# A gated mix of cached attention and an MLP on one core: the last row of wo on each partition is loaded early by GpSimd in seven loads of unequal size

## The chip, the cores and the metric

The kernel runs on one core of one Trainium2 chip. The engines of a core are TensorE (PE in the profile), VectorE (DVE), ScalarE (ACT), GpSimd (POOL) and SyncE (SP); each has its own program, and they meet only at semaphores. Loads from the chip's memory (HBM) are issued by an engine's program and carried out by the core's 16 DMA engines. The metric is the device time of one launch in microseconds.

## The reference

One token attends to a cache of 32,768 positions; 32 query heads share 8 key-value heads, four to one. Beside it a gated MLP runs on the same token, and a sigmoid gate mixes the two. All is float32.

```python
x = A_x                                               # 1 x 1 x 512
g = _sigmoid((x * gate_w).sum(-1, keepdims=True))
q = (x @ wq).reshape(B, Sq, 32, 128)                  # per head
...
scores = jnp.einsum("bhqd,bhkd->bhqk", q, k) * (Dh ** -0.5)
p = _softmax(scores, axis=-1)
o = jnp.einsum("bhqk,bhkd->bhqd", p, v)
a = o.transpose(0, 2, 1, 3).reshape(B, Sq, 4096) @ wo # wo is 4096 x 512
...
b = (_silu(x @ w1) * (x @ w3)) @ w2                   # 512 -> 1792 -> 512
return g * a + (1 - g) * b
```

The two caches hold 2 x 8 x 32,768 x 128 floats, 268 MB; wq and wo hold 8.4 MB each, w1, w2 and w3 3.7 MB each.

## The kernel before

Three buffers of 8 MB, `ra`, `rb` and `rc`, take turns for everything that is loaded. Each has 64 KB on each of the 128 partitions, and a load fills a whole buffer, so each partition gets one piece of 64 KB. SP issues all the large loads in an order written out by hand (lines 133 to 166): wq, w1 and w3 first, then for each of the eight key-value heads two halves of K (into `ra` and `rb`) and two halves of V (into `rc`). Before each load SP waits on a count (`c_k` for scores done, `c_v` for values done) that says that TensorE is through with the buffer's last content.

For each head DVE transposes the K pieces in place (line 368), PE computes the scores (298), ACT copies them out of PSUM (406), PE turns them (322), DVE and PE find the maxima, ACT computes the exponentials into `prob` (412), and in the next turn of the loop PE multiplies them with V (312). The result of a head goes through ACT into `ob`, a tile of 512 floats per partition (409), from where PE sums it with `fold` (332, `heads`). GpSimd's only work in the loop is to place the queries of the next head in `winbuf` (285): it waits until the scores of the head before are done, copies four times, and signals `t_win`, for which PE waits at the start of a turn.

The last stage begins when the last V half has been used. `wo` is seen as 128 partitions with 32 rows of 512 floats each (row 32p + k lies on partition p as its k-th piece). It is loaded into `rc` in two halves of 16 rows, with the semaphores `l_wo0` and `l_wo1` (line 157). w2 follows into `ra` as five loads of 7, 4, 2, and twice half a row (163 and 166, semaphores `l_w20` to `l_w24`). PE runs 32 multiplications with wo (444), waiting for `l_wo0` before the first and `l_wo1` before the 17th, then those with w2 (451 and 423), each group behind its semaphore; between them it adds in the wo part by way of ACT, `ob` and `fold` (477 and 423). DVE and ACT copy the result out of PSUM (485) and ACT stores it (489).

`ob` also holds x at the start of the kernel (`xr`), and the sigmoid of the MLP's gate (268). `prob` is 1,040 floats wide: columns 0 to 511 are the weights of the first V half, 512 to 1023 those of the second.

Of the kernel before, what the change touches and what calls it, by code (L numbers as in the profile page):

```python
# [9 lines left out]
PE, DVE = mybir.EngineType.PE, mybir.EngineType.DVE  # L10

P = 128


class Count:
# [11 lines left out]
@with_exitstack  # L27
def kernel(ctx, tc, x, k_cache, v_cache, wq, wo, w1, w3, w2, gate_w, out):
    nc = tc.nc
    rb, rc = (nc.alloc_sbuf_tensor(n, [P, 16384], F32).ap() for n in ("rb", "rc"))  # L30
    l_q, l_w1, l_w3 = (nc.alloc_semaphore(n) for n in ("l_q", "l_w1", "l_w3"))
    loads = [(rc, wq, l_q)]
    n = w1.shape[0] * w1.shape[1] // P
    loads += [(rb[:, i * n:(i + 1) * n], w, sem) for i, (w, sem) in enumerate(((w1, l_w1), (w3, l_w3)))]
    for to, w, sem in loads:
        i = nc.sync.dma_start(to, w.rearrange("(p c) n -> p (c n)", p=P)).then_inc(sem, 16)

        tc.no_tile_sem_insts.add(i.ins.name)
    tc.close()
    tc.compile()  # L40
    _program(nc, rb, rc, l_q, l_w1, l_w3, x, k_cache, v_cache, wq, wo, w1, w3, w2, gate_w, out)


def _program(nc, rb, rc, l_q, l_w1, l_w3, x, k_cache, v_cache, wq, wo, w1, w3, w2, gate_w, out):
    pe, dve, act, pool, sp = nc.tensor, nc.vector, nc.scalar, nc.gpsimd, nc.sync
    _, HKV, S, DH = k_cache.shape
    D = x.shape[-1]
    F = w1.shape[1]
    HQ = wq.shape[1] // DH
    REP = HQ // HKV  # L50
    NC = D // P
    FR = F // P
    FJ = F // 4
    SCALE = DH ** -0.5
    NK = S // (2 * P)
    W = NK * DH
    assert DH == P and D == 4 * P and REP == 4 and HKV == 8 and NK == 128 and F == FR * P

    def sb(name, *shape):
        return nc.alloc_sbuf_tensor(name, [P, *shape], F32).ap()  # L60

    def token(name):
        return nc.alloc_semaphore(name)

    def count(name):
        return Count(nc, name)
# [9 lines left out]
    winbuf = sb("winbuf", 4 * 32 + 16)  # L76
    sbuf = sb("sbuf", 16, 32, 2)
    prob = sb("prob", 1024 + 16)
    ob = sb("ob", 512)
    otall = sb("otall", REP + HQ)  # L80
    oq = sb("oq", 64)
    gsm, gate = sb("gsm", 1), sb("gate", 2)
# [3 lines left out]
    flat = sbuf.rearrange("p a i m -> p (a i m)")  # L86
    omask = flat[:, 0:P]
    hid = flat[:, P:P + FJ]
    htp = sb("htp", FR, 32)

    xr, gp = ob[0:1, 0:D], flat[0:1, D:2 * D]
    gr = prob[0:1, 0:8 * (D // 8 + 2)].rearrange("o (k d) -> o k d", k=8)[:, :, 0:D // 8]

    zero, row = flat[32:33, 0:D], prob[0:1, 0:D]
# [15 lines left out]
    l_v = [token(f"l_v{i}") for i in range(2)]  # L110
    l_wo = [token(f"l_wo{i}") for i in range(2)]
    l_w2 = [token(f"l_w2{i}") for i in range(5)]

    c_q, c_k, c_v, c_e = (count(n) for n in ("c_q", "c_k", "c_v", "c_e"))
    c_nm, c_act, c_pool, done = token("c_nm"), count("c_act"), count("c_pool"), count("done")
# [10 lines left out]
    def take(sem, n=1, engine=pe):  # L126
        engine.wait_ge(sem, n).then_inc(sem, -n)  # L127
# [4 lines left out]
    half = W // 2  # L132
# [21 lines left out]
    wod = wo.rearrange("(p k) e -> p (k e)", k=32)  # L154
    sp.wait_ge(c_v.sem, 2 * HKV - 2)
    for i in range(2):
        sp.dma_start(rc[:, i * half:(i + 1) * half], wod[:, i * half:(i + 1) * half]).then_inc(l_wo[i], 16)
    w2t = ra[:, 0:FR * D].rearrange("p (k e) -> p k e", e=D)
    w2d = w2.rearrange("(p k) e -> p k e", k=FR)
    W2 = (0, 7, 11, 13, 14)  # L160
# [3 lines left out]
    for i in range(2):  # L164
        e = slice(i * D // 2, (i + 1) * D // 2)
# [36 lines left out]
    @contextmanager  # L202
    def ahead(name, mark, left, right):

        pe.br_lt(left, right, on_true=f"{name}_end", on_false=f"{name}_body").branch_hint(mark)
        with nc.body(f"{name}_body", valid_engines=[PE]):
            yield
            pe.br(f"{name}_end")
        nc.switch_bb(f"{name}_end")
# [3 lines left out]
    for c in range(NC):  # L213
        m = pe.matmul(  # L214
            mc[:, NC + c:NC + c + 1], xr.rearrange("o (p c) -> o c p", c=NC)[:, c], ones[0:1, 0:1],
            start=True, stop=True,
# [8 lines left out]
    for c in range(NC):  # L225
        for b in range(2):
            for j in range(4):
# [3 lines left out]
                    start=(c == 0), stop=(c == NC - 1),  # L231
# [46 lines left out]
    for h in range(HKV):  # L278
        if h:
            pool.wait_ge(c_k.sem, 2 * h)  # L280
        else:
            pool.wait_ge(c_act.sem, n_win)
            pool.wait_ge(c_pool.sem, c_pool.n)
        for r in range(4):
            pool.tensor_copy(  # L285
                winbuf[32 * r:32 * r + 32, 16:144].rearrange("p (c k) -> p c k", k=32)[:, :, 4 * r:4 * r + REP],
                winraw[32 * r:32 * r + 32, h],
            ).then_inc(t_win, 1)


    def scores(m, region, first, last):
# [127 lines left out]
    acc, pb = s_ps[1], s_ps[0]  # L419

    def rows(lhs, rhs, start=False, stop=False, quarters=range(4)):
        for j in quarters:
            i = pe.matmul(  # L423
                pb[32 * j:32 * j + 32, 0:P], lhs, rhs[:, j * P:(j + 1) * P], start=start, stop=stop
            )
        return i
# [11 lines left out]
    with ahead("fifth", marks[4], zero_reg, 0):  # L438
        take(t_e)
        for k in range(32):  # L440
            if k % 16 == 0:
                pe.wait_ge(l_wo[k // 16], 16)
            t = k % 4
            pe.matmul(  # L444
                acc[32 * t:32 * t + 32, :], oq[:, k:k + 32], rc[:, k * D:(k + 1) * D], start=(k < 4), stop=False,
                skip_group_check=True,
            )
        pe.wait_ge(l_w2[0], 16)
        for k in range(W2[1]):
            t = k % 4  # L450
            i = pe.matmul(  # L451
                acc[32 * t:32 * t + 32, :], htp[:, k, :], w2t[:, k, :], start=False, stop=(k >= W2[1] - 4),
                skip_group_check=True,
            )
        i.then_inc(c_e.sem, 1)
        for i in range(1, 3):
            pe.wait_ge(l_w2[i], 16)
            for k in range(W2[i], W2[i + 1]):
                rows(htp[:, k, :], w2t[:, k, :], start=(k == W2[1]))
                if k == W2[2] - 1:  # L460
                    take(t_e)
                    rows(fold, ob)
# [61 lines left out]
```

## Time and profile before

| what | us |
|---|---|
| median of 3 runs | 691.83 (691.78 to 691.87) |
| the profiled execution's own time | 691.74 |
| its span, first to last instruction | 690.4 |
| PE busy | 349.7 |
| DVE busy | 306.9 |
| ACT busy | 41.6 |
| POOL busy | 7.0 |
| bytes moved, mean rate | 296.36 MB, 429 GB/s |

The span is what the trace shows between the first and the last instruction; 1.34 us of the execution's own time lie around it. The first table of the profile gives busy time by engine, a second one the span in 40 slices, where a digit of 9 is a share of 90% or more.

### The profile page before, as it was taken

What the parts mean: (1) busy time and instruction counts of PE and PEld (TensorE: products, weight loads), DVE (VectorE), ACT (ScalarE), POOL (GpSimd) and SP (SyncE); (2) the same over time, 40 slices, a digit from 0 to 9 for tenths busy, and PEclk for the clock granted to TensorE, in tenths of its full rate; (3) what the DMA queues carried; (4) which work ended last, traced back from release to release, by engine and by line L of the source; (5) the groups of instructions that cost most, each with busy time, mean ns of one, the idle gap of its engine ahead of it and who ended that gap; (6) DMA issues with size and microseconds to landing.
All of it is one profiled execution on the core that took longest, in us unless ns stands there. A gap on an engine that the chain in (4) does not pass through costs nothing. (4 is left out here: it accounts for less than half of the span.)

```text
span 690.4 us, 6719 instructions
## 1 busy us (share of the span) xinstructions
PE 349.7 (51%) x2946; PEld 112.6 (16%) x2946; DVE 306.9 (44%) x194; ACT 41.6 (6%) x111; POOL 7.0 (1%) x41
## 2 busy tenths in 40 slices
PE   1721645757065721757066721766075712766567
PEld 1200103103011120203021220203021210203122
DVE  1015862991725447091825447091815446191000
ACT  0110011002000010002000010002000010002000
POOL 0000000000000000000000000000000000000000
PEclk9985675988578965889567965988578965878679
DMA  9999999999999999999999999999999999999997
GB/s 414 393 469 426 425 426 427 444 448 429 426 425 440 425 437 452 429 429 425 437 429 429 456 433 429 425 433 433 425 444 444 430 429 425 437 429 429 452 411 320
DMA packets 6079, 296.36 MB, mean 429 GB/s; under 512 B 691, under 2 KB 947, under 8 KB 1078
## 3 DMA queue, kind: packets, MB, share of 16 engines
q1 hardware_dynamic: 6048, 296.23, 99.3%
q8 instruction: 6, 0.10, 0.1%
q14 instruction: 3, 0.02, 0.0%
q10 hardware_dynamic: 22, 0.01, 0.0%
HBM read 296.23 MB, written 0.00 MB: 429 GB/s over the span
## 5 line engine op out<-in xcount | busy, mean ns | idle before, releaser
L368 DVE STREAM_TRANSPOSE rb<-rb 128x2048 f32<-128x2048 f32 x64 | 141.8, 2275 | 130.7 <-DVEq L127 130.7
L312 PE MATMUL psum<-rc,prob 128*32 128x512 f32 x896 | 114.9, 671 | 140.5 <-PEq L127 140.5
L368 DVE STREAM_TRANSPOSE ra<-ra 128x2048 f32<-128x2048 f32 x64 | 141.3, 2274 | 58.3 <-DVEq L127 58.3
L298 PE MATMUL psum<-rb,winbuf 128*32 128x512 f32 x512 | 88.8, 771 | 84.9 <-PEq L127 84.9
L298 PE MATMUL psum<-ra,winbuf 128*32 128x512 f32 x512 | 60.9, 614 | 26.7 <-PEq L127 21.2
L312 PEld LDWEIGHTS psum<-rc,prob 128*32 128x32 f32 x896 | 34.2, 122 | 216.0 <-issue 216.0
L392 DVE TENSOR_REDUCE mx<-psum 128x4 f32<-128x1024 f32 x8 | 9.8, 1225 | 86.9 <-DVEq L127 86.9
L298 PEld LDWEIGHTS psum<-rb,winbuf 128*32 128x32 f32 x512 | 13.0, 120 | 159.1 <-issue 159.1
L406 ACT COPY sbuf<-psum 128x512 f32<-128x512 f32 x16 | 9.9, 616 | 471.1 <-PE psum L298 471.1
L298 PEld LDWEIGHTS psum<-ra,winbuf 128*32 128x32 f32 x512 | 16.8, 112 | 69.4 <-issue 69.4
L412 ACT ACTIVATE prob<-psum,nm 128x256 f32<-128x256 f32 x32 | 18.8, 693 | 47.0 <-DVE nm L400 47.0
L322 PE MATMUL psum<-ident,sbuf 128*64 128x64 f32 x512 | 18.1, 234 | 5.0 <-PEq L127 5.0
L322 PEld LDWEIGHTS psum<-ident,sbuf 128*64 128x64 f32 x512 | 17.0, 148 | 12.5 <-issue 12.5
L373 DVE SCALAR_TENSOR_TENSOR otall<-psum,gate,recip 128x4 f32 (+1 forms) x8 | 1.7, 214 | 33.3 <-DVEq L127 33.3
L345 PE MATMUL psum<-sums,ones 128*128 128x4 f32 x16 | 4.5, 350 | 22.8 <-PEq L127 22.8
L312 PE MATMUL psum<-rb,prob 128*32 128x512 f32 x64 | 8.8, 714 | 9.4 <-DMA rb<-in_A_v_cache_dram 9.4
L312 PE MATMUL psum<-ra,prob 128*32 128x512 f32 x64 | 9.9, 790 | 3.5 <-DMA ra<-in_A_v_cache_dram 3.5
L285 POOL COPY winbuf<-winraw 32x16 f32<-32x16 f32 x32 | 6.1, 190 | 535.7 <-PE psum L298 501.5
L444 PE MATMUL psum<-rc,oq 128*32 128x512 f32 x64 | 9.0, 712 | 3.9 <-DMA rc<-in_A_wo_dram 3.5
L229 PE MATMUL psum<-rc,xp 128*32 128x512 f32 x64 | 8.4, 687 | 4.7 <-DMA rc<-in_A_wq_dram 4.7
L256 PE MATMUL psum<-rb,xp 128*32 128x448 f32 x64 | 7.8, 637 | 5.4 <-DMA rb<-in_B_w_dram 5.3
L214 PE MATMUL psum<-ones,ob 1*128 1x1 f32 x8 | 2.0, 370 | 15.1 <-DMA prob<-in_gate_w_dram 15.1
(62 smaller groups left out, 86.4 us busy)
## 6 DMA issues: line engine op xcount, KB each, us to landing
rc<-in_A_wo_dram SPq DMA_DIRECT2D x2, 4096.0 KB, 45.8
rb<-in_B_w_dram SPq DMA_DIRECT2D x2, 3584.0 KB, 34.1
ra<-in_B_w_dram SPq DMA_DIRECT2D x1, 1792.0 KB, 33.0
ra<-in_B_w_dram SPq DMA_DIRECT2D x1, 1024.0 KB, 35.2
ra<-in_B_w_dram SPq DMA_DIRECT2D x1, 512.0 KB, 35.9
ra<-in_B_w_dram SPq DMA_DIRECT2D x2, 128.0 KB, 35.7
rc<-in_A_v_cache_dram SPq DMA_DIRECT2D x14, 31.1
ra<-in_A_k_cache_dram SPq DMA_DIRECT2D x8, 41.5
```

The source lines that it names most:

```text
L229: m = pe.matmul(pq[b][32 * j:32 * j + 32, :], xp[:, c, :], rc[:, o:o + REP * DH], start=(c == 0), stop=(c == NC - 1),)
L256: i = pe.matmul(ps[32 * j:32 * j + 32, 0:FJ], xp[:, c, :], rb[:, o:o + FJ], start=(c == 0), stop=(c == NC - 1))
L285: pool.tensor_copy(winbuf[32 * r:32 * r + 32, 16:144].rearrange("p (c k) -> p c k", k=32)[:, :, 4 * r:4 * r + REP], winraw[32 * r:32 * r + ...
L298: i = pe.matmul(s_ps[m][32 * g:32 * g + 32, :], winbuf[:, w:w + 32], region.rearrange("p (n c i) -> p c n i", c=4, i=32)[:, c, n:n + 16], ...
L312: i = pe.matmul(o_ps[32 * t:32 * t + 32, :], prob[:, w:w + 32], region[:, n * DH:(n + 4) * DH], start=(r == 0 and g == 0 and f == 0), stop ...
L322: i = pe.matmul(pf[64 * s:64 * s + 64, 64 * a:64 * a + 64], sbuf[:, a].rearrange("p i m -> p (i m)"), ident.rearrange("p (gf r s q) -> p s ...
L345: pe.matmul(mc[:, 0:REP], ones, sums, start=True, stop=True).then_inc(t_n, 1)
L368: dve.transpose(part[:, c], part[:, c]).then_inc(t_tr, 1)
L392: dve.tensor_reduce(mx, pf.rearrange("p (a q) -> p q a", q=REP), axis=AX.X, op=ALU.max).then_inc(t_mx, 1)
L406: act.copy(sbuf[:, :, :, m], s_ps[m].rearrange("p (n i) -> p n i", i=32)).then_inc(t_ev, 1)
L412: act.activation(prob[:, 0:1024].rearrange("p (a n q) -> p n a q", a=16, q=REP)[:, :, :, q], pf.rearrange("p (n a q) -> p n a q", n=16, q= ...
L444: pe.matmul(acc[32 * t:32 * t + 32, :], oq[:, k:k + 32], rc[:, k * D:(k + 1) * D], start=(k < 4), stop=False, skip_group_check=True,)
```

## The change

The last of the 32 rows of wo on each partition is no longer loaded by SP with the second half: that load shrinks from 16 rows to 15. The row goes into a tile of its own, `wx`, of 2 x 264 floats per partition of which 2 x 256 are used, so that it arrives there as two pieces of 1 KB per partition. GpSimd issues this load, after its `winbuf` copies for the third head, as seven loads of 3, 34, 2, 34, 5, 34 and 16 partitions, all of which signal the semaphore `l_g`. The last of PE's 32 multiplications with wo waits for `l_g` and reads `wx`.

To make room, `ob` becomes the second half of `prob`, and x at the start moves into the scores' buffer `sbuf`. The number of bytes loaded is the same.

```diff
+SHARES = (3, 34, 2, 34, 5, 34, 16)
...
-    ob = sb("ob", 512)
+    ob = prob[:, 512:1024]
...
+    wx = sb("wx", 2, 264)[:, :, 0:256]
-    xr, gp = ob[0:1, 0:D], flat[0:1, D:2 * D]
+    xr, gp = flat[0:1, 0:D], flat[0:1, D:2 * D]
...
+    l_g = token("l_g")
...
     sp.wait_ge(c_v.sem, 2 * HKV - 2)
     for i in range(2):
-        sp.dma_start(rc[:, i * half:(i + 1) * half], wod[:, i * half:(i + 1) * half]).then_inc(l_wo[i], 16)
+        k = slice(16 * i * D, (16 + 15 * i) * D)
+        sp.dma_start(rc[:, k], wod[:, k]).then_inc(l_wo[i], 16)
...
+        if h == 2:
+            first = 0
+            for n in SHARES:
+                pool.dma_start(
+                    wx[first:first + n],
+                    wo.rearrange("(p k) (a e) -> p k a e", k=32, a=2)[first:first + n, 31],
+                ).then_inc(l_g, 16)
+                first += n
+            assert first == P
...
+            if k == 31:
+                pe.wait_ge(l_g, 16 * len(SHARES))
             t = k % 4
             pe.matmul(
-                acc[32 * t:32 * t + 32, :], oq[:, k:k + 32], rc[:, k * D:(k + 1) * D], start=(k < 4), stop=False,
-                skip_group_check=True,
+                acc[32 * t:32 * t + 32, :], oq[:, k:k + 32], rc[:, k * D:(k + 1) * D] if k < 31 else wx,
+                start=(k < 4), stop=False, skip_group_check=True,
             )
```

On GpSimd, the loop over the eight heads is written out; these rows are its copies into `winbuf`, four for each head, before (-) and now (+). Sizes are partitions by row by elements.

```order
-L285 COPY winbuf<-winraw 32x4x4 x32
...
+L289 COPY winbuf<-winraw 32x4x4 x12
+L296 DMA wx<-in_A_wo_dram 3x2x256
+L296 DMA wx<-in_A_wo_dram 34x2x256
+L296 DMA wx<-in_A_wo_dram 2x2x256
+L296 DMA wx<-in_A_wo_dram 34x2x256
+L296 DMA wx<-in_A_wo_dram 5x2x256
+L296 DMA wx<-in_A_wo_dram 34x2x256
+L296 DMA wx<-in_A_wo_dram 16x2x256
+L289 COPY winbuf<-winraw 32x4x4 x20
```

The seven loads stand between the copies for the third head and those for the fourth.

On TensorE, the last stage before, from the first multiplication with wo (`rc`) to the first group with w2 (`ra`); a name in brackets is a semaphore that the row waits for.

```order
L444 MATMUL psum<-rc,oq 32x512 [waits t_e,l_wo0]
L444 MATMUL psum<-rc,oq 32x512 x15
L444 MATMUL psum<-rc,oq 32x512 [waits l_wo1]
L444 MATMUL psum<-rc,oq 32x512 x15
L451 MATMUL psum<-ra,htp 32x512 [waits l_w20]
```

The same place now:

```order
L459 MATMUL psum<-rc,oq 32x512 [waits t_e,l_wo0]
L459 MATMUL psum<-rc,oq 32x512 x15
L459 MATMUL psum<-rc,oq 32x512 [waits l_wo1]
L459 MATMUL psum<-rc,oq 32x512 x14
L459 MATMUL psum<-wx,oq 32x512 [waits l_g]
L466 MATMUL psum<-ra,htp 32x512 [waits l_w20]
```

The count and order of the multiplications are unchanged; the 32nd has a wait of its own, for GpSimd's loads.

## Rows read from the trace of the kernel before

**Rows 1.** The page: span, DMA totals.

```profile
span 690.4 us, 6719 instructions
...
DMA packets 6079, 296.36 MB, mean 429 GB/s; under 512 B 691, under 2 KB 947, under 8 KB 1078
...
q1 hardware_dynamic: 6048, 296.23, 99.3%
```

**Rows 2.** DMA view, 120 to 660 us: packets, MB, share of 16 engines.

```profile
DMA packets 4033, 233.92 MB, mean 433 GB/s; under 512 B 448, under 2 KB 448, under 8 KB 448
...
q1 hardware_dynamic: 4030, 233.90, 100.1%
q14 instruction: 3, 0.02, 0.0%
```

**Rows 3.** Windows at the end: us, engines, PEclk, DMA share, GB/s.

```profile
685.50:686.00 0.50, 0.50 (x7) 0.12 (x3) 0.00 (x0) 0.00 (x0) 0.00 (x0) 1.00 0.98 371
686.00:686.25 0.25, 0.25 (x6) 0.00 (x0) 0.00 (x0) 0.00 (x0) 0.00 (x0) 1.00 0.92 340
686.25:686.50 0.25, 0.25 (x6) 0.00 (x0) 0.00 (x0) 0.00 (x0) 0.00 (x0) 1.00 0.75 279
686.50:686.75 0.25, 0.25 (x11) 0.23 (x12) 0.00 (x0) 0.00 (x0) 0.00 (x0) 1.00 0.47 176
686.75:687.00 0.25, 0.25 (x19) 0.25 (x15) 0.00 (x0) 0.22 (x1) 0.00 (x0) 1.00 0.48 184
687.00:687.25 0.25, 0.25 (x20) 0.25 (x13) 0.00 (x0) 0.25 (x1) 0.00 (x0) 1.00 0.34 123
687.25:687.50 0.25, 0.25 (x16) 0.11 (x5) 0.00 (x0) 0.11 (x1) 0.00 (x0) 1.00 0.34 119
687.50:687.75 0.25, 0.25 (x12) 0.16 (x8) 0.00 (x0) 0.00 (x0) 0.00 (x0) 1.00 0.26 90
687.75:688.00 0.25, 0.25 (x17) 0.25 (x13) 0.00 (x0) 0.00 (x0) 0.00 (x0) 1.00 0.09 29
```

**Rows 4.** DMA view, 67 to 69 us.

```profile
q1 hardware_dynamic: 16, 1.05, 122.6%
q8 instruction: 1, 0.02, 3.2%
```

**Rows 5.** DMA view, 101 to 118 us, then 660 to 668 us.

```profile
q8 instruction: 3, 0.05, 1.1%
...
q8 instruction: 1, 0.02, 0.8%
```

**Rows 6.** Chain of waits, its pieces in order of time: start, us, what.

```profile
672.50 3.64 PE psum L444 x32
676.14 3.49 another core or an unknown queue
679.63 0.04 issue
679.67 5.34 PE psum L444 x32
685.01 1.71 PE psum L451 x14
686.72 1.91 PE psum L423 x59
```

**Rows 7.** Waits from 660 us on: engine, line, releaser, us in total, times, longest.

```profile
PE psum L444 <- DMA rc<-in_A_wo_dram: 3.5, 1, 3.5
...
PEld psum L423 <- DMA ra<-in_B_w_dram: 0.7, 1, 0.7
```

**Rows 8.** DMA view, 686.3 to 687.9 us, the last rows of w2.

```profile
q1 hardware_dynamic: 184, 0.23, 39.1%
```

**Rows 9.** DMA view, 7 to 13 us, ACT's small loads beside SP's.

```profile
q10 hardware_dynamic: 17, 0.00, 0.3%
```

**Rows 10.** Timeline of GpSimd: start, us, what, idle before and releaser.

```profile
156.90 0.93 POOL L285 COPY winbuf<-winraw 32x16 f32<-32x16 f32 x4 [56.51 <-PE psum L298]
234.30 0.93 POOL L285 COPY winbuf<-winraw 32x16 f32<-32x16 f32 x4 [76.46 <-PE psum L298]
```

**Rows 11.** DMA issues: ACT's gate load in the timeline, SP's V loads.

```profile
3.42 0.73 ACTq L170 DMA_DIRECT2D prob<-in_gate_w_dram  x1
...
rc<-in_A_v_cache_dram SPq DMA_DIRECT2D x14, 31.1
```

**Rows 12.** Windows of 3.4 us up to the end, columns as in Rows 3.

```profile
677.40:680.80 3.40, 1.13 (x12) 0.42 (x16) 0.00 (x0) 0.00 (x0) 0.00 (x0) 1.00 0.99 419
680.80:684.20 3.40, 3.40 (x20) 0.87 (x16) 0.00 (x0) 0.00 (x0) 0.00 (x0) 0.51 0.95 399
684.20:687.60 3.40, 3.40 (x58) 1.44 (x54) 0.00 (x0) 0.58 (x1) 0.00 (x0) 0.99 0.77 300
```

## The prediction

> **What bounds the kernel now.** Start with the page: 296 MB in a span of 690.4 us, and SP's queue alone keeps the 16 DMA engines 99.3% busy, while PE has work for half the span [rows 1]. The DMA view of the long middle says it more sharply: from 120 to 660 us the queue fills 100.1% of 16 engines [rows 2]. No engine of the 16 is ever without work there, so nothing that PE, DVE or ACT do in the loop can cost or bring time, and a DMA engine that falls behind its neighbours is never given the chance to catch up: there is no pause in which the others wait for it.
>
> Next, the windows at the end, where the streams run out [rows 3]. Read the DMA share times 16 as the number of engines that still move data: 16 up to 686 us, 12 in the second quarter after it, 7 or 8 from 686.5 on, five between 687.0 and 687.5, four, and the last ends at about 687.9 (0.09 of the last quarter). The engines, which all carry the same large loads, finish 1.5 to 1.9 us apart. Five of them are a group of their own.
>
> The trace names a cause. Between 67 and 69 us one instruction fetch of 16 KB takes 3.2% of 16 engines for 2 us, that is 1.02 us of one engine [rows 4]; three more between 101 and 118 us take 1.1% of 16 x 17, 1.0 us each, and one just after 666 us takes 0.8% of 16 x 8, again 1.0 us [rows 5]. Five fetches of a microsecond each, and five engines that end about a microsecond after the rest: I read the late group as those five engines, on the assumption that each fetch met another engine. Three fetches on another queue in the middle [rows 2] are of half the size.
>
> Last, what the end of the program hangs on. In the chain PE stands still for 3.49 us until the second half of wo has landed (679.63), then runs without a large gap to 688.62 [rows 6]; the waits confirm that wo is what it stood for, and that it stood 0.7 us for the second load of w2 [rows 7]. A load has landed only when the last of its engines is done, so both releases are set by the late group.
>
> **The change part by part.** Bytes are the same; what changes is which DMA engine carries them and when.
>
> *SP's second half of wo* loses one row in 16: 256 KB, 16 KB for each engine. In [rows 4] 1.05 MB took 122.6% of 16 x 2 us, or 39.2 us of engine time: 26.8 KB per us. Each engine saves 16.4/26.8 = 0.61 us just ahead of the end.
>
> *The rows come back through GpSimd*, in pieces of 1 KB. The nearest pieces are w2's last rows: 0.23 MB in 39.1% of 16 x 1.6 us, 23 KB per us [rows 8], so a row of 2 KB costs 0.089 us. Each of the seven loads also has to signal. ACT's small packets beside SP's stream took 0.3% of 16 x 6 us for 17 of them, 0.017 us each [rows 9]; seven such on one engine are at most 0.12 us, none if it takes no part in a load; I take 0.06. That stream went on beside them, so I take no cost for the change of queue.
>
> An engine with r of the 128 rows therefore changes by -0.61 + 0.06 + 0.089 r: -0.55 us with none, +0.16 with an even 8, and it breaks even at 6. What counts is how many rows the five late engines get. No row of the trace shows how a load of 34 partitions is cut. I assume: into as many equal parts as divide its count, up to 16, each part on the next engine in turn. Then 3, 34, 2, 34, 5, 34 make 3 + 2 + 2 + 2 + 5 + 2 = 16 parts, once around, and the load of 16 gives each engine one row more. Ten engines get 2 rows (-0.37 us), six get 18 (+1.05 us). [...]
>
> If the five late engines are all among the ten, they end at 687.9 - 0.37 = 687.53. The six with more would be early ones, gone between 686.1 and 686.5 before, and end between 687.15 and 687.55. The sizes fit: 1.42 us between the two kinds against the 1.5 us or so that the groups lie apart. So the end moves by 0.37 us, and PE with it: its wait for wo is still over 2.5 us long and ends 0.37 us sooner, and everything behind starts from there.
>
> *Moving work earlier* delays the six engines by about 1.65 us from 160 us on. SP's V loads land 31.1 us after they are issued [rows 11] and one load of 8.39 MB takes 19.6 us at 429 GB/s [rows 1], so some 11 us of work are queued ahead of each; the delay leaves no engine idle. A load in the middle lands by up to 0.2 us later (two rows and signals on an engine that is already last); the last of them hides behind the 3.49 us.
>
> *GpSimd's time*: it issues seven loads after 157.8 us, and behind them stand the copies for the fourth head, for whose signal PE waits; before, these stood ready for 76.46 us until 234.30 [rows 10]. At ACT's 0.73 us an issue [rows 11] the seven take 5 us; even at 10 us each they would fit. *The wait for `l_g`* has had 500 us. *`ob` in `prob`*: the copy into it follows the values that read it, and the exponentials that overwrite it follow the maxima, which PE works out after the sums; the order of the engines is what it was, and the DMA-bound loop would hide a microsecond anyway. These cost nothing.
>
> Sum against the profiled execution: 691.74 - 0.37 = **691.4**. The median lies 0.09 above that execution; against it the same sum is 691.46. What a measurement of this kernel can tell from no change is about 0.2%, 1.4 us, so this is no change by that measure. No cut could exceed it: the shares in [rows 3] add up to 0.91 us of all engines' work after 686.0, so a perfectly even finish would come at 686.9, 1.0 us sooner.
>
> **The rivals.**
>
> *A heavy part falls on a late engine.* The rows do not name engines. Were the six drawn blindly, at least one would meet the five late ones in 94 of 100 draws; only the fit of the sizes speaks against it. Then the end comes at 687.9 + 1.05, the time is **692.8**, slower by 0.15%. It decides as soon as one engine with 18 rows was among the last five; one that is late by a small fetch (0.3 us) would give about 691.7.
>
> *The loads are cut otherwise*, and the change doesn't do what it says. Spread evenly, each engine is 0.16 us worse: 691.9. Cut into pieces of three rows from the first engine on, 34 fills 11 engines and puts a row on a twelfth; the first two get 13 rows, the next nine 10 to 12, the last four one. A late engine with 13 rows gives -0.55 + 1.16 = +0.61, 692.35; if all late ones were among those with one row the gain would be 0.46, 691.3. [...]
>
> *GpSimd's pieces cost far more.* A 16 KB fetch took 1.02 us where SP's rate gives 0.61. If each of the 36 pieces on a heavy engine lost that 0.4 us, it would end 14 us late, beside 705; from 0.05 us extra for a piece (36 x 0.05 = 1.8, of which 0.4 is the room to 687.9) the loss passes 0.2%. The small packets at the start [rows 9] show nothing of the kind.
>
> [...]
>
> **How the numbers follow.** The forecast gets 0.55; a heavy part on a late or half-late engine 0.25; another cut 0.11; the pieces' cost 0.04; the clock 0.02; the rest 0.03. The likeliest is 691.4. The range runs from 690.9, beyond the best cut (691.2 with no rows on the late engines), to 692.9, the first rival with 0.1 for the spread of executions; it leaves out the costlier pieces and the unforeseen. Only those pass 0.2%: faster 0.03, slower 0.06, within 0.91.
>
> **What would show each step.** In the windows at the end, the share should hold near 16 engines for longer and then fall faster: five engines alone for half a microsecond must be gone, and the last end lie near 687.5. GpSimd's queue should show 256 packets of 1 KB and some 0.089 us of engine time per row, soon after 157 us. PE's wait for wo should end 0.2 to 0.4 us sooner. If a few engines trail by a microsecond or more behind the others, a heavy part met a late engine. If the end stays as it was, the loads were cut evenly. A span of 700 us would mean that the pieces cost what fetches do. A different set of fetches, or fetches that meet other engines from run to run, would make the whole sum wrong, and the times of the new kernel would then scatter by more than the 0.1 us of the old.

## The result, and the profile after

The changed kernel takes 695.02 us (median of 6 runs, 694.57 to 695.18) against 691.85 (691.78 to 692.1): 3.17 us more, a ratio of 1.0044 with a 95% interval of 1.0031 to 1.0057. The forecast was 691.4 in a range up to 692.9. The profiled execution took 694.65 us, 2.91 more than that of before, and its span is 693.2.

The page, span and DMA queues of the changed kernel, beside [rows 1]:

```profile
span 693.2 us, 6726 instructions
...
DMA packets 6687, 296.36 MB, mean 428 GB/s; under 512 B 1219, under 2 KB 1475, under 8 KB 1686
...
q1 hardware_dynamic: 6048, 295.96, 99.2%
q0 software_dynamic: 608, 0.27, 0.1%
```

The bytes are the same, SP's queue is as full as before, and GpSimd's queue (q0) takes a tenth of a per cent. Nothing looks wrong, except that the mean rate has lost 1 GB/s: the same bytes took longer while the engines were never idle. So the packets themselves must have become slower, somewhere. The timeline of GpSimd and the DMA issues say where to look:

```profile
158.48 5.24 POOL L296 DMA_DIRECT2D wx<-in_A_wo_dram  x7
236.95 0.93 POOL L289 COPY winbuf<-winraw 32x16 f32<-32x16 f32 x4 [73.22 <-PE psum L311]
```

```profile
wx<-in_A_wo_dram POOLq DMA_DIRECT2D x3, 68.0 KB, 56.4
wx<-in_A_wo_dram POOLq DMA_DIRECT2D x1, 32.0 KB, 86.1
```

The seven issues take 5.24 us, but the last load lands only 86 us later. The DMA view of this stretch, 158 to 248 us, first before, then after (packets, MB, share of 16 engines):

```profile
q1 hardware_dynamic: 656, 38.80, 99.6%
```

```profile
q1 hardware_dynamic: 634, 37.36, 98.7%
q0 software_dynamic: 602, 0.27, 1.1%
```

Divide engine time by bytes. Before, 99.6% of 16 x 90 us for 38.80 MB is 36.97 us of one engine per MB; after, 98.7% for 37.36 MB is 38.04. SP's packets are 3% slower as long as GpSimd's loads run beside them, (38.04 - 36.97) x 37.36 / 16 = 2.5 us for each engine. I call this figure the *loss beside the loads*. The shares are printed to a tenth of a per cent, so it is good to about 0.1 us, and a loss below that is none. From 260 to 640 us the two traces agree to the packet rate (100.1% both, 433 GB/s both). GpSimd's own packets take 1.1% of 90 us, 1.0 us, of which SP's shorter load gives 0.61 back. Together 2.5 + 1.0 - 0.61 = 2.9 us, the whole of the 2.91.

At the end, the windows that answer to [rows 3]:

```profile
688.00:688.50 0.50, 0.50 (x6) 0.00 (x0) 0.00 (x0) 0.00 (x0) 0.00 (x0) 1.00 1.02 401
...
689.00:689.25 0.25, 0.00 (x0) 0.00 (x0) 0.00 (x0) 0.25 (x1) 0.00 (x0) 1.00 0.65 246
689.25:689.50 0.25, 0.16 (x8) 0.16 (x12) 0.00 (x0) 0.15 (x1) 0.00 (x0) 1.00 0.76 279
689.50:689.75 0.25, 0.25 (x16) 0.25 (x12) 0.00 (x0) 0.00 (x0) 0.00 (x0) 1.00 0.63 221
689.75:690.00 0.25, 0.25 (x19) 0.25 (x12) 0.00 (x0) 0.00 (x0) 0.00 (x0) 1.00 0.43 152
690.00:690.25 0.25, 0.25 (x18) 0.25 (x14) 0.00 (x0) 0.00 (x0) 0.00 (x0) 1.00 0.23 78
690.25:690.50 0.25, 0.25 (x16) 0.12 (x6) 0.00 (x0) 0.00 (x0) 0.00 (x0) 1.00 0.07 25
```

The plateau of five engines is gone: from 689.5 us on there are 10 engines, then 7, 4, and from 690.25 on one alone (0.07 x 16), which moves its last packets after 690.5. The five no longer trail as a group, but one engine does.

### The profile page after: what moved, and what is told of

Read it like the earlier page. It is cut to its first block, busy times and chain, and to the rows that moved or that the text cites. A ratio compares the mean times of both kernels' runs of the same rounds, so it can differ in the third digit from the quotient of the medians.

```text
span 693.2 us, 6726 instructions
## 1 busy us (share of the span) xinstructions
PE 354.0 (51%) x2946; PEld 112.7 (16%) x2946; DVE 306.9 (44%) x194; ACT 41.6 (6%) x111; POOL 12.2 (2%) x48
## 3 DMA queue, kind: packets, MB, share of 16 engines
q1 hardware_dynamic: 6048, 295.96, 99.2%
## 5 line engine op out<-in xcount | busy, mean ns | idle before, releaser
L311 PE MATMUL psum<-ra,winbuf 128*32 128x512 f32 x512 | 62.6, 627 | 26.7 <-PEq L130 21.0
L218 PE MATMUL psum<-ones,sbuf 1*128 1x1 f32 x8 | 2.0, 370 | 15.2 <-DMA prob<-in_gate_w_dram 15.2
```

What stands on the lines that cost most here:

```text
L311: i = pe.matmul(s_ps[m][32 * g:32 * g + 32, :], winbuf[:, w:w + 32], region.rearrange("p (n c i) -> p c n i", c=4, i=32)[:, c, n:n + 16], ...
```

## The experiments

Two theories stood against each other at first: the delay comes with GpSimd's queue, by its packets or its loads, or it comes with something in the data. A table of all runs follows the single ones. The loss beside the loads is worked out as above, over 158 to 248 us unless another stretch is named. Code cuts show the lines that matter; "..." marks what is left out.

**The shared buffer alone.** From the kernel before:

```diff
-    ob = sb("ob", 512)
+    ob = prob[:, 512:1024]
-    xr, gp = ob[0:1, 0:D], flat[0:1, D:2 * D]
+    xr, gp = flat[0:1, 0:D], flat[0:1, D:2 * D]
```

> The kernel before with only the second part of the change: ob is the second half of prob, x lies in sbuf at the start; wo is loaded by SP as before, nothing by GpSimd. If the loss is GpSimd's loads alone: 691.85, within 0.2 of before. If the shared buffer puts a wait between ACT and PE that matters: up to the full 695.0. Anything between would split the 3.17 us between the two parts.

691.88 against 691.82, ratio 1.0 (0.9991 to 1.0009). The buffer costs nothing that can be measured; the loss comes with the loads.

**One load of 128 partitions by GpSimd.**

```diff
-SHARES = (3, 34, 2, 34, 5, 34, 16)
+SHARES = (128,)
```

> As the change, but GpSimd loads the row in one load of 128 partitions, the same 256 pieces of 1 KB. In the change the trace has 608 packets on GpSimd's queue, 38 for each of the 16 DMA engines, while SP's 64 KB packets beside them took 2.49 us instead of 2.42. Theory of the packets: every packet of that queue, data or filler, costs SP's stream on its engine 0.07 us; one load should make about 5 packets for each engine, so 0.35 us, and 8 rows for each engine 0.16: 692.3. Theory of the loads: 2.7 us over seven loads, 0.38 us for one: 692.4, the same. Theory of the bytes: the same pieces of 1 KB from GpSimd cost the same, 694.5 to 695.0. Theory of the uneven shares (a heavy engine ends last): the loss goes, 692.0, but so it would by packets; the number of packets and the length of SP's packets beside them must tell.

691.95, ratio 1.0001 (0.9992 to 1.001). DMA view, 158 to 248 us:

```profile
q1 hardware_dynamic: 655, 38.73, 99.5%
q0 software_dynamic: 80, 0.26, 0.8%
```

80 packets are 5 for each engine, four of two rows and a signal. The loss is 0.07 us, within the error of the figure: the same bytes in the same 1 KB pieces from the same queue cost SP's stream nothing that can be seen. The theory of the bytes is dead, and 5 packets should by the theory of the packets have cost 0.35.

**One load of 128 partitions by ACT**, with GpSimd's loop over the shares taken out:

```diff
-SHARES = (3, 34, 2, 34, 5, 34, 16)
+SHARES = (128,)
...
             ).then_inc(t_p, 1)
+        if h == 1:
+            act.dma_start(wx, wo.rearrange("(p k) (a e) -> p k a e", k=32, a=2)[:, 31]).then_inc(l_g, 16)
```

> As the change, but the row is loaded in one load of 128 partitions by ACT's queue, after the second head's exponentials, and nothing is issued by GpSimd. Theory of the packets on GpSimd's queue: ACT's queue makes no fillers, 8 rows cost each engine about what its share of SP's load did: 691.9 to 692.1. If any second queue beside SP's costs 0.07 us for each of its packets, and each 1 KB piece is one packet, 16 pieces and a signal cost 1.2 us: 693.0. Theory of the bytes (1 KB pieces are dear whoever issues them): 694.5 or more.

692.05, ratio 1.0002 (0.9993 to 1.0011).

```profile
q1 hardware_dynamic: 655, 38.73, 99.5%
q10 hardware_dynamic: 272, 0.26, 0.8%
```

The loss is 0.07 us again. ACT's queue (q10) makes one packet of each 1 KB piece, 256, and 16 signals. A second queue as such costs nothing that can be seen.

**Eight loads of 16 partitions by GpSimd.**

```diff
-SHARES = (3, 34, 2, 34, 5, 34, 16)
+SHARES = (16,) * 8
```

> As the change, but GpSimd's seven loads become eight of 16 partitions each; every engine gets one row from each load. Theory of the packets: one packet with two pieces and one signal from each load, 16 for each engine, 1.1 us, and 0.16 for the even share: 693.1. Theory of the loads: 8 x 0.38 = 3.0 us: 695.0. Theory of the bytes: 694.5 to 695.0.

694.17, ratio 1.0037 (1.0023 to 1.0051), between the forecasts of the packets (693.1) and of the loads (695.0).

```profile
q1 hardware_dynamic: 640, 37.75, 99.5%
q0 software_dynamic: 256, 0.26, 0.9%
```

256 packets, fewer than half of the change's 608, cost nearly as much: a loss of 2.3 us, 0.29 for each load. Not packets, then. What is left is the number of loads, or a third theory: *which* engine writes *where*. I assume that in a load of 128 partitions each of the 16 engines has the partitions that it also has in SP's loads, and that in loads of 16 or 34 neighbours it has others; the traces name no engines, so no run shows this. 0.29 us is about what an engine needs for 8 KB, a quarter of such a load, at the 26.8 KB per us of [rows 4] (0.31); why a quarter should count, no run shows. The next four runs set the theory of the places against the others.

**The same shares from ten loads.**

```diff
-SHARES = (3, 34, 2, 34, 5, 34, 16)
+SHARES = (3, 17, 17, 2, 17, 17, 5, 17, 17, 16)
```

> As the change, but each load of 34 partitions is cut into two of 17; by the cut read from the change's trace, each of the six heavy engines still gets the same 18 rows and the others 2, now from ten loads. Theory of the packets: nine data or filler packets for each load of 17, 68 for each engine with the signals instead of 38; at 0.07 us each 4.8 us instead of 2.7: 697.1. Theory of the loads (0.3 to 0.4 us for each load queued behind another): ten instead of seven, 696.1. Theory of the places (an engine writes to partitions that another engine's stream serves, and the two delay each other; the same rows go to the same places): 695.0, as the change.

695.01, ratio 1.0049 (1.0035 to 1.0062): as the change. These loads last longer, so here is the stretch from 158 to 318 us, first before, then the change, then this run:

```profile
q1 hardware_dynamic: 1184, 69.21, 99.9%
```

```profile
q1 hardware_dynamic: 1161, 67.70, 99.4%
```

```profile
q1 hardware_dynamic: 1157, 67.44, 99.1%
```

Packets went from 608 to 1,088 and loads from seven to ten, and the loss over this stretch only from 2.7 to 2.8 us.

**Twice as many pieces.**

```diff
-    wx = sb("wx", 2, 264)[:, :, 0:256]
+    wx = sb("wx", 4, 132)[:, :, 0:128]
...
-                    wo.rearrange("(p k) (a e) -> p k a e", k=32, a=2)[first:first + n, 31],
+                    wo.rearrange("(p k) (a e) -> p k a e", k=32, a=4)[first:first + n, 31],
```

> As the change, with the same seven loads, but the row arrives in four pieces of 512 B on each partition instead of two of 1 KB, so GpSimd makes twice as many pieces; packets of up to 4 KB should stay 38 for each engine. Theory of the packets or of the loads: 695.0, as the change. Theory of the pieces (each piece or filler piece, about 117 for each engine, costs 0.023 us): 2.5 us more, 697.5. Theory of the places: 695.0, plus 0.3 for the smaller pieces.

695.42, ratio 1.0055 (1.0042 to 1.0069): 0.4 us over the change, not 2.5.

```profile
q1 hardware_dynamic: 628, 36.96, 98.5%
```

The loss is 3.3 us in place of 2.5, so smaller pieces do cost SP's stream something, but doubling them adds a third and not the whole once more. Most of the loss is not paid for pieces.

**Eight loads, each of all 128 partitions** and 64 of the 512 columns, in place of the loop over the shares:

```diff
+            wl = wo.rearrange("(p k) (c e) -> p k c e", k=32, c=8)
+            for j in range(8):
+                pool.dma_start(
+                    wx[:, j // 4, j % 4 * 64:j % 4 * 64 + 64], wl[:, 31, j],
+                ).then_inc(l_g, 16)
```

> Eight loads by GpSimd as in the run with eight of 16, but each takes all 128 partitions and 64 of the 512 columns, 256 B per partition. [...] Theory of the loads, or of the packets with 2 KB each: 694.2, as with eight of 16, or more for the small pieces. Theory of the places: no delay of SP's packets; the pieces of 256 B cost an engine some 0.4 us more than pieces of 1 KB: 692.0 to 692.5.

692.48, ratio 1.0009 (1.0 to 1.0018), within the forecast of the places, 1.7 us under eight loads of 16. That each engine writes here where it writes for SP's loads is the assumption above.

```profile
q1 hardware_dynamic: 646, 38.14, 98.5%
q0 software_dynamic: 256, 0.26, 0.9%
```

The same eight loads, 256 packets and bytes as above, with a loss of 0.5 us in place of 2.3. This rules out the number of loads. The 0.5 may be the pieces of 256 B, which this run has and the run with one load has not; no run separates it.

**Eight loads of every eighth partition,** in the same place:

```diff
+            wl = wo.rearrange("(p k) (a e) -> p k a e", k=32, a=2)
+            for j in range(8):
+                pool.dma_start(wx[j:P:8], wl[j:P:8, 31]).then_inc(l_g, 16)
```

> Eight loads of 16 partitions as in the run with eight of 16, the same pieces, packets and engines, but each load takes every eighth partition instead of 16 neighbours. Theory of the loads or packets: 694.2, unchanged. Theory of the places: in the run with 16 neighbours SP's packets beside each load lost 0.29 us, what an engine needs for 8 KB. [...]

693.07, ratio 1.0018 (1.0009 to 1.0027), 1.1 us under the 694.2 of the loads and the packets.

```profile
q1 hardware_dynamic: 644, 38.01, 98.6%
q0 software_dynamic: 256, 0.26, 0.8%
```

The loss is 0.9 us, less than half of that with 16 neighbours, with nothing changed but which partitions, and with them which rows of wo, go together.

**Eight loads of 16 neighbours by ACT.** As ACT's one load, with

```diff
+            wl = wo.rearrange("(p k) (a e) -> p k a e", k=32, a=2)
+            for j in range(8):
+                act.dma_start(wx[16 * j:16 * j + 16], wl[16 * j:16 * j + 16, 31]).then_inc(l_g, 16)
```

> The eight loads of 16 neighbouring partitions, but issued by ACT's queue after the second head's exponentials; GpSimd issues nothing. ACT's one load of 128 gave 692.05, GpSimd's eight of 16 gave 694.17. Theory of the places (which engine writes to which partitions, whoever issues the load): SP's packets lose 0.29 us beside each load, 694.2. Theory of GpSimd's queue (its packets, signals or its way of handing out work are what delays SP's stream): 692.1.

695.43, ratio 1.0051 (1.0037 to 1.0065).

```profile
q1 hardware_dynamic: 628, 36.96, 98.7%
q10 hardware_dynamic: 384, 0.26, 0.9%
```

A loss of 3.4 us, with no load issued by GpSimd: the delay is not its queue's. ACT pays more than GpSimd for the same loads. Its 384 packets are 24 for each engine instead of 16, one for each 1 KB piece and eight signals; whether that is why was not tried.

**A single load of 34, by ACT and by GpSimd,** on top of the kernel with the shared buffer, into a tile that nothing reads; PE's 32nd multiplication waits for it:

```diff
+            act.dma_start(wx[0:34], wo.rearrange("(p k) (a e) -> p k a e", k=32, a=2)[0:34, 31]).then_inc(l_g, 16)
```

and for GpSimd the same with `pool.dma_start`, behind its third group of copies.

> The kernel with the shared buffer, all 32 rows of wo loaded by SP as before; ACT loads the last row of the first 34 partitions a second time, in one load, into a tile that nothing reads. By the cut read from the traces two engines get 17 rows each, 1.5 us of work, the others nothing. If these two are early engines the end moves by up to 0.4 us, if one is a late engine by 1.5. [...] Theory of GpSimd's fillers (in the change, the 14 engines without data got a filler packet for each data packet): ACT makes none, SP's packets keep their length but for a few beside the two engines: 692.2 to 693.4.

> The same extra load of the first 34 partitions, issued by GpSimd where the change issues its seven. Both theories expect the delay of the change here, a third of 2.7 us on every engine, 0.8 to 0.9, beside the two engines' own 1.5: 692.7 to 694.2. The difference to the run with ACT's load is what GpSimd's fillers add: none by the places, 0.8 us by the fillers.

692.78 by ACT (1.0015, 1.0006 to 1.0024) and 692.62 by GpSimd (1.0012, 1.0003 to 1.0021). ACT's load first, then GpSimd's, 158 to 248 us:

```profile
q1 hardware_dynamic: 655, 38.73, 99.9%
q10 hardware_dynamic: 68, 0.07, 0.2%
```

```profile
q1 hardware_dynamic: 654, 38.67, 99.9%
q0 software_dynamic: 160, 0.07, 0.3%
```

The packets of GpSimd's run by size, and its load from issue to landing:

```profile
DMA packets 6239, 296.43 MB, mean 429 GB/s; under 512 B 833, under 2 KB 1089, under 8 KB 1238
```

```profile
wx<-in_A_wo_dram POOLq DMA_DIRECT2D x1, 68.0 KB, 28.6
```

GpSimd's load makes 160 packets, 10 for each of 16 engines, though 34 rows can't fill them: 142 are under 512 B (833 against the 691 of [rows 1]), signals and fillers, and 18 hold the data. ACT's makes 70, the 68 pieces and two signals; the two that this stretch lacks come after it. The loss is 0.4 us with ACT and 0.6 with GpSimd, so the fillers add some 0.2, hardly more than the error, and not 0.8. A load of 34 lost less than the 0.8 that the theory of the places had put down, and the median fell just outside its range for GpSimd.

**Other addresses in HBM.** One rival to the places in SBUF was left: rows of neighbouring partitions lie 64 KB apart in HBM, so the loads of 16 also differ in what they read. The run with eight loads of 16, with

```diff
-                    wo.rearrange("(p k) (a e) -> p k a e", k=32, a=2)[first:first + n, 31],
+                    wo.rearrange("p (a e) -> p a e", a=2)[first:first + n],
```

> GpSimd's eight loads of 16 neighbouring partitions once more, with the same destinations, pieces and packets, but from other addresses: each load reads 16 rows of wo that lie one behind the other in HBM (32 KB in one stretch) instead of 16 rows that are 64 KB apart. wx so holds other rows of wo than the product needs; this alone is changed. Theory of the places in SBUF: 694.2, as with the rows 64 KB apart, since the same engines write to the same partitions. Rival: what collides are the reads, 16 engines at once at addresses 64 KB apart; then the delay goes and the time is 691.9 to 692.2.

693.97, ratio 1.0033 (1.0021 to 1.0046).

```profile
q1 hardware_dynamic: 640, 37.75, 99.0%
q0 software_dynamic: 256, 0.26, 0.9%
```

The loss is 1.9 us against 2.3: most of it stays when the addresses read change and the places written don't.

| run | time, us | over before, us | packets beside SP's | loss beside the loads, us |
|---|---|---|---|---|
| the change | 695.02 | 3.17 | 608 | 2.5 |
| shared buffer alone | 691.88 | 0.06 | 0 | 0 |
| GpSimd, 1 of 128 | 691.95 | 0.13 | 80 | 0.07 |
| ACT, 1 of 128 | 692.05 | 0.23 | 272 | 0.07 |
| GpSimd, 8 of 16 neighbours | 694.17 | 2.35 | 256 | 2.3 |
| GpSimd, ten loads (158 to 318 us) | 695.01 | 3.24 | 1,088 | 2.8 |
| GpSimd, pieces of 512 B | 695.42 | 3.65 | 608 | 3.3 |
| GpSimd, 8 of 128 | 692.48 | 0.71 | 256 | 0.5 |
| GpSimd, 8 of every eighth | 693.07 | 1.30 | 256 | 0.9 |
| ACT, 8 of 16 neighbours | 695.43 | 3.60 | 384 | 3.4 |
| ACT, 34 extra | 692.78 | 0.95 | 70 | 0.4 |
| GpSimd, 34 extra | 692.62 | 0.79 | 160 | 0.6 |
| GpSimd, 8 of 16, other addresses | 693.97 | 2.12 | 256 | 1.9 |

Read the last two columns down: the loss goes with the time and not with the packets (the two runs with 34 extra also move 68 KB more). For ACT's eight loads of 16 the sum made for the change gives 3.4 + 0.8 - 0.6 = 3.6 us, as measured. One load of 128 partitions is free from either queue, and eight of 128 cost little; loads of neighbouring partitions cost from either queue, wherever they read.

No run points to a version that beats the kernel before: the one load of 128 partitions ends level with it, and every cut into fewer partitions that was tried lost time.

## Why the prediction was wrong

**The bound** was read rightly. DMA engines that never pause can't hide a delay, and so 2.5 us lost around 200 us still stood at the end, 450 us later.

**The cut**, an assumption in the prediction, was read rightly too, though not as the 256 packets of 1 KB that were expected. 160 packets for a load of 34 are nine and a signal for each engine; 17 rows at two rows to a packet make nine, and twice nine are the 18 with data. So the packets of a load of 34 fit two engines with 17 rows each. Shares of three rows, as in the second rival, would have made two packets and a signal on an engine; no load here was cut so. Which engines got the heavy parts, and whether the parts went to the engines in turn, no trace says. The five late engines are gone as a group, but the loss moved every engine's end, so whether the heavy parts stayed clear of them stays open.

**The price of a row** held: in the run with one load, GpSimd's packets take 0.8% of 16 x 90 us for 128 rows, 0.09 us a row as estimated. In the change its queue takes 1.0 us of each engine in place of the 0.77 that 8 rows and 0.06 make; the rest is fillers and signals, which I had at 0.06.

**The step that failed** is the sentence "That stream went on beside them, so I take no cost for the change of queue." The 17 small packets of [rows 9] were too few to show a cost, and they raised a question about the queue where the question was about the places. Loads of neighbouring partitions delay SP's packets, whichever queue issues them (eight of 16 by 2.3 us from GpSimd and by 3.4 from ACT); the change has three of 34 and one of 16 above all, and its loads cost 2.5 us per engine where I had put nothing. The rival of the costly pieces came nearest: it named 0.05 us a piece as the point from which the loss passes 0.2%. But it put the price on the six heavy engines' pieces, by likeness to an instruction fetch, and the run with twice the pieces and the one with ten loads show that pieces set a lesser part of the loss and packets hardly any.

**The gain from the late engines**, 0.37 us in the sum, came out near nothing: an average engine accounts for 2.9 of the 2.91 us, so the last engine ends as far behind the average as before. The five no longer trail, but one does; the trace does not say by name which engine it is.

**The small terms** held. Seven issues took 5.24 us for an estimated 5, and behind them the copies for the fourth head were ready 73.22 us early. `ob` in `prob` costs nothing (691.88).

**The path to the end** was another than forecast. PE came to wo at 677.15 us, where it had come at 672.50 before [rows 6], and no longer stood still for it; the chain of waits now runs through w2's load. PE's granted clock was 0.50 from 676 to 682.8 us (in the kernel before 0.51 from 680.8 to 684.2 [rows 12]), and yet PE still waited 0.58 us for w2's second load, which arrived late with the stream, so the clock did not set the end:

```profile
654.04 35.25 DMA ra<-in_B_w_dram
```

```profile
676.00:679.40 3.40, 2.85 (x14) 1.19 (x18) 0.22 (x2) 0.00 (x0) 0.00 (x0) 0.50 1.01 434
679.40:682.80 3.40, 3.40 (x20) 0.92 (x16) 0.00 (x0) 0.00 (x0) 0.00 (x0) 0.50 0.90 383
```

```profile
677.15 9.45 PE L459 MATMUL psum<-rc,oq 128*32 128x512 f32 x59 [0.38 <-PEq L130]
...
689.34 1.08 PE L436 MATMUL psum<-ra,htp 128*32 128x128 f32 x32 [0.58 <-DMA ra<-in_B_w_dram]
```

**What stays open.** That the partitions which a load covers decide is shown by the runs with 8 of 128, every eighth partition, ACT's 8 of 16 and the other addresses. Why they do is not shown. One reading is that an engine is slow, and slows others, where it writes to partitions that another engine's stream fills. The other is that many engines' rows of one load crowd into few places at once; the load of 128, as assumed above, does neither. The smaller loss with every eighth partition speaks for crowding; the single load of 34 by GpSimd, on two engines only, speaks against it, since it lost about as much for its bytes (0.6 us for 68 KB) as eight loads of 16 (2.3 for 256). Loads of 16 that leave each engine with the partitions of its stream would separate the two and were not tried. What makes a place, and which partitions belong to one, no run shows: only two patterns of 16 partitions were tried, with 0.29 us a load for neighbours and 0.9 / 8 = 0.11 for every eighth. About a sixth of the loss went with the addresses (1.9 against 2.3). And the change loses 2.5 us on the average engine although 256 KB are only 16 KB or 0.6 us per engine. Had the six heavy engines that the prediction counts alone carried this loss, it would be 6.7 us for each, and they would trail by more than the some 2 us within which all 16 end; so the delay spreads to engines with few of the rows, and why was not tried.

## What to carry to other kernels

When one queue keeps all DMA engines busy, ask of every added load not only how many bytes each engine gets, but which partitions the load covers. Here 256 KB in loads of 16 or 34 neighbouring partitions cost the stream 2.3 to 2.5 us, where the same 256 KB in one load of all 128 cost 0.07, no more than the error. A loss of this kind shows in no idle time and no busy share (SP's queue filled 99.2% of the engines after and 99.3% before); divide a queue's engine time by its bytes, stretch by stretch, and compare. And a price taken from a few small packets that happen to lie beside a stream says nothing on what moves there at another place.

## What the runs showed of the hardware

- Small loads beside a full stream landed late. The single load of 34 by GpSimd, ten packets for each engine, landed 28.6 us after its issue, and ACT's one load of 128, 17 for each engine, after 41.1. SP's 64 KB packets beside them took about 2.4 us each (99.9% of 16 x 90 us for 38.67 MB), so one of these before each small packet would be 24 and 41 us: an estimate, as the traces do not show the order of the packets. The change's loads of 34, which stood behind other loads in their queue, took 56.4 us (the median of three).
- A load of 34 rows by GpSimd makes 160 packets, of which 18 hold the data; the other 142, under 512 B, are as many as nine fillers for each of 14 engines and a signal for each of the 16. On ACT's queue it makes 70, one for each piece and two signals.
- Eight loads of 16 neighbouring partitions slowed a full stream whether GpSimd (2.3 us) or ACT (3.4 us) issued them. The loss was less than half (0.9) when the 16 partitions lay eight apart, and nothing of it was seen (0.07) in one load of all 128 from either queue.
